# Batch 0's first MLP pass in another order, with three squares on GpSimd ahead of its loads

## The chip, the cores and the metric

The kernel runs on one core of a Trainium2 chip. The metric is the device time of one execution in microseconds (us); smaller is better. The engines are TensorE (PE in the profile; PEld is its weight load), VectorE (DVE), ScalarE (ACT), GpSimd (POOL) and SyncE (SP). Each works through its own instructions in the order in which they were recorded, and waits for the others through semaphores.

## The reference

A chunked attention (4 batches, 8 heads, 768 rows of 64) feeds an MLP with a snake activation on all 3072 tokens of width 512; the inner width is 2048.

```python
for c in range(nc):                       # 24 chunks of 32 queries, context 16 left, 8 right, 8 memory rows
    scores = scale * np.matmul(q_c, k_full.transpose(0, 1, 3, 2))
    ...
    out[:, :, c_start:c_end] = np.matmul(a, v_full)
...
h = x @ w_in
s = np.sin(alpha * h)
g = h + s * s / (alpha + 1e-09)
return (g @ w_out).astype(np.float32)
```

## The kernel before

The work runs in five stages. Stage -1 makes the attention of batch 0. Stage i (0 to 3) computes the MLP of batch i and, beside it, the attention of batch i+1. Nothing is scheduled at run time: the order is written out by hand in `WORDS`, one string of short words for each stage, and each word records its instructions at the end of the queues of the engines it uses. This case is about `WORDS[1]`, that is stage 0, up to the first scores of batch 1.

The MLP of a batch has two passes. The first pass makes 16 tiles of `gT`, each 128 of the 2048 inner columns for 768 tokens. For tile a the words are:

- `b a` and `h a`: the tile's eight matmuls (line 471, 128x384, in two halves of four) into a pair of PSUM banks; `h` then issues the sine on ScalarE (line 486, into a buffer `u`).
- `q aV`, `q aA`, `q aP`: the square of the sine on VectorE (line 494), ScalarE (line 491) or GpSimd (line 494), into a buffer `s2`.
- `g a`: the finish on VectorE (line 498), which writes the tile of `gT` and gives the two banks back.

The second pass is a series of matmuls of `gT` with `w_out_sb` (line 509, 128x512). Word `f n` takes the next n of them from a feed; they are used as fillers of PE. `o8` puts them in the feed in groups of eight: the first 16 are tiles 0 to 7 for token block 0 and then for block 1, so the third needs rows of `w_out` that belong to tile 2 and the fifth those of tile 4. While not all 16 tiles are finished, the feed gives 16 at the most.

Batch 1's attention needs q and k with the head dimension on the partitions. `l hp` and `k hp` turn one head pair on PE (line 322, 12 transposes of 128 columns) into one bank, and `L hp`, `K hp` copy it out on the engine that the last letter names (lines 342 and 333). `s61` is the first pair of score matmuls (line 428), `v0` the first value matmuls (line 457).

The loads of this stage are issued by GpSimd: `I7g` (w_in, line 250), `Uxy` (tiles x to y-1 of `w_out`, line 256; digits above 9 are letters, so `Ube` is tiles 11 to 13), `dq108` and `dk108` (q and k of batch 1, line 192), and `V158`, `V125`, `V102` (v of batch 1, lines 209 and 216). GpSimd runs its squares and issues its loads from the same queue. The loads share eight semaphores (lanes DMASW0 to DMASW7) in turn, so an issue waits until the load eight places before it has landed.

Of the kernel before, what the change touches and what calls it, by code (L numbers as in the profile page):

```python
# [26 lines left out]
    ),  # L27
    (
# [5 lines left out]
    ),  # L34
    (
# [887 lines left out]
```

## Time and profile before

| | us |
|---|---|
| median of 3 runs | 212.74 (212.47 to 213.02) |
| the profiled execution | 213.16 |
| its span, first to last instruction | 211.0 |
| PE busy in the span | 204.2 |
| ACT, DVE and POOL busy | 142.5, 139.8 and 101.4 |

The profile is of one execution, and its span leaves out 2.16 us of start and end (213.16 less 211.0). The profiled execution is 0.42 us above the median, about the spread of the runs. The granted TensorE clock was 1.000 over the span. A matmul's end is modelled, so PE counts as busy while matmuls follow each other; how closely they follow is read from the starts.

### The profile page before, as it was taken

To read this page: it belongs to the slowest core of one execution; us is meant where nothing else is said; L and a number is where in the kernel's file an instruction comes from. 1 tells how busy PE (TensorE), PEld (TensorE's weight loads), DVE (VectorE), ACT (ScalarE), POOL (GpSimd) and SP (SyncE) were. 2 spreads that over 40 slices of the span, in tenths; PEclk is the share of its full clock that TensorE was granted. 3 is DMA by queue.
4 is the path that set the end of the run, shared out by engine and by line. 5 is a ranking of instruction groups with operands and counts; after the bars stand their busy time and mean duration, and the time that the engine had idled before them with its cause. 6 is when DMAs were issued, how large, how long until landed. Compare 5 with 4: busy or idle time off the path is not lost.

```text
span 211.0 us, 4425 instructions
## 1 busy us (share of the span) xinstructions
PE 204.2 (97%) x1695; PEld 114.1 (54%) x1695; DVE 139.8 (66%) x212; ACT 142.5 (68%) x228; POOL 101.4 (48%) x144
## 2 busy tenths in 40 slices
PE   7988999999999999999999999999999999999994
PEld 2566565655455565554456555554555565554443
DVE  7688698997363669958685569887347289964011
ACT  4597798959837579969817398968765198991110
POOL 8999609497695496029991058960000023300000
PEclk9999999999999999999999999999999999999999
DMA  6999999999999699999996359999235400000312
GB/s 208 309 150 159 205 207 204 205 163 173 180 142 147 139 150 148 143 146 139 160 176 118 76 149 147 166 145 56 99 93 121 137 3 0 2 0 3 149 50 99
DMA packets 96452, 27.79 MB, mean 132 GB/s; under 512 B 84896, under 2 KB 92976, under 8 KB 96432
## 3 DMA queue, kind: packets, MB, share of 16 engines
q0 software_dynamic: 69824, 13.65, 87.2%
q1 hardware_dynamic: 25520, 12.30, 27.2%
q10 hardware_dynamic: 1088, 1.57, 2.2%
q8 instruction: 13, 0.21, 0.5%
q14 instruction: 7, 0.06, 0.1%
HBM read 29.66 MB, written 6.29 MB: 170 GB/s over the span
## 4 chain that ended last, share of the span: by engine, by line
PE 77%; DVE 9%; ACT 6%; issue 4%; DMA 2%; POOL 1%; SPq 0%; DVEq 0%; ACTq 0%
PE ps L509 40%; PE ps L471 28%; DVE gT L498 4%; PE ps L457 3%; DVE s L494 3%; PE ps L428 2%; DMA kq_f<-in_k_dram 2%; ACT u L486 2%; PE ps L409 1%; ACT qT L342 1%; PE ps L322 1%; DVE x_blk L397 1%; POOL s L494 1%; ACT s L491 1%; ACT pt L375 1%
## 5 line engine op out<-in xcount | busy, mean ns | idle before, releaser
L509 PE MATMUL ps<-w_out_sb,gT 128*128 128x512 bf16 (+2 forms) x400 | 89.1, 371 | 0.0
L471 PE MATMUL ps<-xT,w_in_sb 128*128 128x384 bf16 x512 | 86.4, 326 | 0.5 <-DVE gT L498 0.2
L498 DVE SCALAR_TENSOR_TENSOR gT<-s,inv_alpha,ps 128x768 bf16<-128x768 f32 x64 | 63.1, 1012 | 11.6 <-POOL s L494 5.3
L471 PEld LDWEIGHTS <-w_in_sb 128*128 128x128 bf16 x512 | 49.6, 98 | 35.4 <-issue 2.6
L486 ACT ACTIVATE u<-ps,alpha_sb 128x768 f32<-128x768 f32 x64 | 56.6, 895 | 17.1 <-PE ps L471 16.7
L509 PEld LDWEIGHTS <-gT 128*128 128x128 bf16 x400 | 36.6, 98 | 37.8 <-DVE gT L498 0.2
L494 POOL TENSOR_TENSOR s<-u 128x768 f32<-128x768 f32 x11 | 17.8, 1620 | 69.7 <-ACT u L486 57.6
L442 ACT ACTIVATE pt<-ps,biasm 128x256 bf16<-128x256 f32 x72 | 27.2, 489 | 10.5 <-PE ps L428 10.5
L516 DVE COPY o_sb<-ps 128x512 f32<-128x512 f32 (+1 forms) x15 | 10.1, 678 | 28.4 <-PE ps L509 26.5
L494 DVE TENSOR_TENSOR s<-u 128x768 f32<-128x768 f32 x24 | 22.9, 953 | 7.6 <-ACT u L486 7.6
L491 ACT ACTIVATE s<-u 128x768 f32<-128x768 f32 x29 | 24.2, 841 | 0.5
L397 DVE TENSOR_TENSOR x_blk<-ps,rinv 96x512 bf16<-96x512 f32 x32 | 22.0, 687 | 1.2 <-DVE rinv L396 0.2
L516 ACT COPY o_sb<-ps 128x512 f32<-128x512 f32 (+1 forms) x10 | 5.6, 562 | 22.3 <-PE ps L509 22.3
L396 DVE RECIPROCAL rinv<-ps 96x8 f32<-96x8 f32 x32 | 6.4, 199 | 13.4 <-PE ps L457 12.5
L209 POOL DMA_DIRECT2D vw<-in_v_dram x13 | 11.8, 911 | 5.3 <-PE ps L409 5.3
L275 POOL DMA_DIRECT2D kst<-in_k_dram x16 | 12.2, 762 | 1.5 <-DMA vw<-in_v_dram 1.1
L216 POOL DMA_DIRECT2D vw<-in_v_dram x13 | 12.4, 955 | 0.0
L269 POOL DMA_DIRECT2D kst<-in_k_dram x16 | 11.1, 691 | 2.0 <-DMA vw<-in_v_dram 1.1
L412 ACT COPY xT<-ps 128x384 bf16<-128x384 bf16 x11 | 5.4, 496 | 8.8 <-PE ps L409 8.7
L282 POOL DMA_DIRECT2D q_bf<-in_q_dram x12 | 10.7, 904 | 0.0
L457 PEld LDWEIGHTS <-pt 128*128 128x128 bf16 x192 | 8.2, 97 | 4.2 <-ACT pt L442 0.3
L765 ACT ACT_TABLE_LOAD x6 | 7.7, 1283 | 3.0 <-issue 2.9
(84 smaller groups left out, 139.1 us busy)
## 6 DMA issues: line engine op xcount, KB each, us to landing
out_dram<-o_sb SPq DMA_DIRECT2D x23, 256.0 KB, 2.3
q_bf<-in_q_dram POOLq DMA_DIRECT2D x12, 128.0 KB, 5.4
w_in_sb<-in_moe_w_in_dram POOLq DMA_DIRECT2D x1, 1152.0 KB, 11.2
vw<-in_v_dram POOLq DMA_DIRECT2D x8, 112.0 KB, 6.2
vw<-in_v_dram POOLq DMA_DIRECT2D x7, 128.0 KB, 6.1
kst<-in_k_dram POOLq DMA_DIRECT2D x14, 64.0 KB, 4.3
kst<-in_k_dram POOLq DMA_DIRECT2D x14, 56.0 KB, 4.6
kq_f<-in_q_dram ACTq DMA_DIRECT2D x2, 384.0 KB, 4.6
```

Of the source, the lines that this page charges most:

```text
L216: nc.gpsimd.dma_start(vw[72:128, c0:hi, 0:D], win(vflat, base + QW * c0 + 48, hi - c0, 56))
L275: nc.gpsimd.dma_start(kst[72:72 + n, j, :].rearrange("p (h d) -> p h d", d=D), k[b, :, QW * j + 48:QW * j + 48 + n, :].rearrange("h p d -> ...
L397: nc.vector.tensor_tensor(out=x_blk[:].rearrange("p g e d -> p e g d"), in0=otv[0:QW, :, :, 0:D], in1=rinv[:].unsqueeze(3).to_broadcast([Q ...
L442: nc.scalar.activation(pt[:, 0:H * QW].rearrange("p (g e c) -> p g e c", g=2, e=4)[:, :, :, 32 * m:32 * m + 32], sc[:, :, 0:4 * QW].rearra ...
L457: nc.tensor.matmul(otv[:, e, hp, :], pt[:, QW * i:QW * i + P], vws[b % 2][:, 2 * hp + e, j, 0:D + 1],)
L471: nc.tensor.matmul(t["hT"][:, hf, 0:HALF], w_in_sb[:, kt, P * t["ft"]:P * t["ft"] + P], t["xT"][:, kt, HALF * hf:HALF * hf + HALF], start= ...
L486: nc.scalar.activation(t["u"][:], t["hT"][:, :, 0:HALF], ACTF.Sin, scale=alpha_sb[:, ft:ft + 1])
L491: nc.scalar.activation(s2[:], u[:], ACTF.Square)
L494: e.tensor_tensor(out=s2[:], in0=u[:], in1=u[:], op=ALU.mult)
L498: nc.vector.scalar_tensor_tensor(out=gT[:, ft, :].rearrange("p (e c) -> p e c", e=2), in0=t["s2"][:], scalar=inv_alpha[:, ft:ft + 1], in1= ...
L509: nc.tensor.matmul(o[:, c0:c1], gT[:, ft, P * s:P * s + P], w_out_sb[:, ft, c0:c1], start=(ft == 0), stop=(ft == FT - 1),)
L516: copier(state["engines"][state["o"] % len(state["engines"])])(o_sb[:, c0:c1], o[:, c0:c1])
```

## The change

Only the first five lines of `WORDS[1]` change; the rest of the stage and all other stages keep their words. Two lines of the diff show the kind:

```diff
-        'o8 b0 h0 I7g q0V U69 U12 b1 h1 dq108 q1A b2 h2 b3 g0 h3 b4 g1 dk108 q2V g2 q3A b5 h5 h4 b6 h6 Ufg g3 '
+        'b0 h0 b3 o8 h3 I7g q3A q0V b1 h1 g0 U69 g3 q1V b2 h2 q2A b4 U12 h4 q4A dq108 b5 dk108 g1 h5 Ufg g2 g4 U01 U56 '
...
```

The tiles come in the order 0 3 1 2 4 5 6 10 7 9 13 8 11 12 15 14 (before: 0 1 2 3 5 4 6 7 10 9 8 11 13 15 12 14). GpSimd squares tiles 6, 7 and 13 (before: 4, 7 and 13). VectorE squares 4 tiles instead of 6 and ScalarE 9 instead of 7. ScalarE still makes 5 of the copies after turns, and VectorE 3. SP's queue is the same, the loads are issued in the same order, and from `f16` before the first scores on PE has the same order as before.

On GpSimd the change stands between the loads of `w_out` and v. The names are: line 256 loads of `w_out` (the fourth row below, of 2x512, is `U24`, and the later one of 512 is `U45`), lines 209 and 216 v (`V158`), line 494 a square; in brackets the semaphores it waits for. Before:

```order
L256 DMA w_out_sb<-in_moe_w_out_dram 128x512 [waits DMASW7_49]
L494 TENSOR_TENSOR s_602<-u 128x768 [waits DVE_49,Activation_49,Pool_49]
L256 DMA w_out_sb<-in_moe_w_out_dram 128x2x512 [waits DMASW0_49]
L494 TENSOR_TENSOR s_630<-u 128x768 [waits DMAHW4_49,Activation_49]
L256 DMA w_out_sb<-in_moe_w_out_dram 128x512 [waits DMASW1_49]
L209 DMA vw_89<-in_v_dram 64x24x64 [waits DMASW2_49]
L216 DMA vw_89<-in_v_dram 56x24x64 [waits DMASW3_49]
L494 TENSOR_TENSOR s_701<-u 128x768 [waits Activation_49]
L256 DMA w_out_sb<-in_moe_w_out_dram 128x3x512 [waits DMASW4_49]
```

And the same stretch of GpSimd's queue after the change:

```order
L256 DMA w_out_sb<-in_moe_w_out_dram 128x512 [waits DMASW7_49]
L494 TENSOR_TENSOR s_619<-u 128x768 [waits DMAHW2_49,Activation_49,Pool_49]
L494 TENSOR_TENSOR s_644<-u 128x768 [waits DVE_49,Activation_49]
L256 DMA w_out_sb<-in_moe_w_out_dram 128x2x512 [waits DMASW0_49]
L494 TENSOR_TENSOR s_671<-u 128x768 [waits Activation_49]
L256 DMA w_out_sb<-in_moe_w_out_dram 128x512 [waits DMASW1_49]
L209 DMA vw_89<-in_v_dram 64x24x64 [waits DMASW2_49]
L216 DMA vw_89<-in_v_dram 56x24x64 [waits DMASW3_49]
L256 DMA w_out_sb<-in_moe_w_out_dram 128x3x512 [waits DMASW4_49]
```

`U24` now stands behind the squares of tiles 6 and 7, and `U45` and `V158` behind that of tile 13, which stood behind them.

On PE the 8 turns (96 transposes) and the 16 fillers ahead of the first scores are dealt out differently. Before: 48 transposes after the 13th tile, 7 fillers 20 matmuls of tiles later, 48 transposes, 9 fillers. After: 24 transposes after the 12th tile, 24 after the 14th, then 5 fillers, 12, 12 and 24 transposes among the last two tiles, and 11 fillers. The five fillers of the change on PE, with the transposes of k ahead of them and those of q behind:

```order
L322 MATMUL ps<-ident,k_bf 64x128
L509 LDWEIGHTS gT [waits DMASW6_49]
L509 MATMUL ps<-w_out_sb,gT 128x512 [waits DVE_49]
L509 LDWEIGHTS gT
L509 MATMUL ps<-w_out_sb,gT 128x512 [waits DMASW2_49]
L509 LDWEIGHTS gT
L509 MATMUL ps<-w_out_sb,gT 128x512 [waits DMASW0_49]
L509 LDWEIGHTS gT
L509 MATMUL ps<-w_out_sb,gT 128x512
L509 LDWEIGHTS gT
L509 MATMUL ps<-w_out_sb,gT 128x512 [waits DMASW1_49]
L322 LDWEIGHTS q_bf
```

In before the same five rows, with the same waits, stand behind tile matmuls:

```order
L471 MATMUL ps<-xT,w_in_sb 128x384
L509 LDWEIGHTS gT [waits DMASW6_49]
L509 MATMUL ps<-w_out_sb,gT 128x512 [waits DVE_49]
L509 LDWEIGHTS gT
L509 MATMUL ps<-w_out_sb,gT 128x512 [waits DMASW2_49]
L509 LDWEIGHTS gT
L509 MATMUL ps<-w_out_sb,gT 128x512 [waits DMASW0_49]
L509 LDWEIGHTS gT
L509 MATMUL ps<-w_out_sb,gT 128x512
L509 LDWEIGHTS gT
L509 MATMUL ps<-w_out_sb,gT 128x512 [waits DMASW1_49]
```

What moved is their place: 124 matmuls of tiles stand ahead of the first filler before, 112 after the change, with 48 transposes ahead in both. The lane DMASW0 is that of `U24` and DMASW1 that of `U45`.

8 rows, old and new, of the table WORDS are left out of this document.

## The prediction

> **What bounds the kernel now.** I read the busy times of two stretches first, to see which engine never rests and whether a delay before the first scores of batch 1 can be made up later; then PE's timeline in the pass that changes; then GpSimd's timeline and the landing of its loads.
>
> ```profile
> 23.29:50.99 27.70, 27.53 (x241) 16.39 (x239) 24.31 (x29) 23.97 (x30) 16.99 (x20) 1.00 1.40 195
> 51.00:205.00 154.00, 153.69 (x1165) 83.30 (x1165) 96.45 (x134) 102.37 (x175) 62.16 (x72) 1.00 1.09 111
> ```
>
> Behind the stretch stands its length, then the busy time of PE (with the number of its instructions), PEld, DVE, ACT and POOL. PE is the one that never rests. From 51 to 205 us PE idles 0.31 us of 154, so what PE loses before 51 us has next to nothing to hide in: I carry it to the end in full. (Since a matmul's end is modelled, short waits are covered by its tail; but those for finishes depend on PE's own tiles and move along with them.) The stretch that changes is 23.29 to 50.99, from the tiles' matmuls to the first score matmul, 27.70 us.
>
> ```profile
> 23.29 16.91 PE L471 MATMUL ps<-xT,w_in_sb 128*128 128x384 bf16 x101
> 40.12 1.30 PE L322 MATMUL ps<-ident,q_bf 128*64 128x128 bf16 x36
> 41.23 0.53 PE L322 MATMUL ps<-ident,k_bf 128*64 128x128 bf16 x12
> 41.87 3.46 PE L471 MATMUL ps<-xT,w_in_sb 128*128 128x384 bf16 x20
> 45.17 1.67 PE L509 MATMUL ps<-w_out_sb,gT 128*128 128x512 bf16 x7
> 46.68 0.81 PE L471 MATMUL ps<-xT,w_in_sb 128*128 128x384 bf16 x4
> 47.42 0.86 PE L322 MATMUL ps<-ident,k_bf 128*64 128x128 bf16 x24
> 48.12 0.50 PE L322 MATMUL ps<-ident,q_bf 128*64 128x128 bf16 x12
> 48.45 0.50 PE L322 MATMUL ps<-ident,k_bf 128*64 128x128 bf16 x12
> 48.89 2.17 PE L509 MATMUL ps<-w_out_sb,gT 128*128 128x512 bf16 x9
> 50.99 0.51 PE L428 MATMUL ps<-qT,kT 64*128 64x96 bf16 x16
> ```
>
> Paces, from start to start. A tile matmul: the undisturbed run below of 58 lasts 9.59 us, of which 0.33 is the tail of the last, so 9.26/57 = 0.1625 us. A filler: 7 in 1.67 with a tail of 0.38, 0.215 us. A transpose: 24 in 0.86 with a tail of 0.22, 0.028 us.
>
> ```profile
> 23.78 9.59 PE L471 MATMUL ps<-xT,w_in_sb 128*128 128x384 bf16 x58
> ...
> 39.71 0.49 PE L471 MATMUL ps<-xT,w_in_sb 128*128 128x384 bf16 x2
> ```
>
> Changing the kind of matmul costs too: the two of the second row start at 39.71 and 39.87, the next could start at 40.03, and the transposes start at 40.12 (above): 0.09 us.
>
> The 27.70 us are then 125 tile matmuls x 0.1625 = 20.31, 96 transposes x 0.028 = 2.69, 16 fillers x 0.215 = 3.44: 26.44 us of bare work. The other 1.26 us are 7 changes of kind (0.63) and 0.63 us of waits. Of these the run of 101 holds 0.33 (16.91 less the tail is 16.58, against 100 x 0.1625 = 16.25), where a tile waits for two banks from a finish; most of the rest lies at 41.87, where a tile waits for a bank of q turns to be copied out (12 transposes from 41.23 and a change end at 41.66). So the order has at the most 0.63 us of waiting to give, 0.3% of the time.
>
> **The loads that the fillers need.**
>
> ```profile
> 21.26 0.90 POOL L192 DMA_DIRECT2D q_bf<-in_q_dram  x1
> 22.14 0.90 POOL L192 DMA_DIRECT2D k_bf<-in_k_dram  x1
> ...
> 24.77 1.06 POOL L256 DMA_DIRECT2D w_out_sb<-in_moe_w_out_dram x2 [1.18 <-DMA w_in_sb<-in_moe_w_in_dram]
> 31.98 1.59 POOL L494 TENSOR_TENSOR s<-u 128x768 f32<-128x768 f32 x1 [6.14 <-ACT u L486]
> 33.53 0.77 POOL L256 DMA_DIRECT2D w_out_sb<-in_moe_w_out_dram x1
> 34.39 1.46 POOL L494 TENSOR_TENSOR s<-u 128x768 f32<-128x768 f32 x1
> 35.81 0.59 POOL L256 DMA_DIRECT2D w_out_sb<-in_moe_w_out_dram x1
> 36.40 0.99 POOL L209 DMA_DIRECT2D vw<-in_v_dram x1
> 41.22 1.82 POOL L494 TENSOR_TENSOR s<-u 128x768 f32<-128x768 f32 x1 [2.83 <-ACT u L486]
> 42.99 2.12 POOL L256 DMA_DIRECT2D w_out_sb<-in_moe_w_out_dram x3
> ```
>
> These are q and k of batch 1, U01 and U56 (24.77, two issues in 1.06 us, the second at 25.3), U24 (33.53), U45 (35.81), V158 (36.40) and Ube with two more (42.99), with the three squares between. Their landings, by DMA issues of short windows in the order of issue (q, k, U01 and U56, U24, U45, V158's first, Ube; the last number is us from issue to landing, of a row with x2 the median):
>
> ```profile
> q_bf<-in_q_dram POOLq DMA_DIRECT2D x1, 768.0 KB, 15.5
> k_bf<-in_k_dram POOLq DMA_DIRECT2D x1, 768.0 KB, 18.5
> w_out_sb<-in_moe_w_out_dram POOLq DMA_DIRECT2D x2, 128.0 KB, 17.2
> w_out_sb<-in_moe_w_out_dram POOLq DMA_DIRECT2D x1, 256.0 KB, 10.9
> w_out_sb<-in_moe_w_out_dram POOLq DMA_DIRECT2D x1, 128.0 KB, 9.4
> vw<-in_v_dram POOLq DMA_DIRECT2D x1, 192.0 KB, 10.4
> w_out_sb<-in_moe_w_out_dram POOLq DMA_DIRECT2D x1, 384.0 KB, 5.6
> ```
>
> So U56 lands at about 25.3 + 17.2 = 42.5, U24 at 33.53 + 10.9 = 44.4, U45 at 35.81 + 9.4 = 45.2, V158 from 36.40 + 10.4 = 46.8. They land in the order of issue whatever the issue time: the queue is backed up by 9 to 17 us. In before the fillers start at 45.17, after U24, and the fifth needs U45 at 45.17 + 4 x 0.215 = 46.03: no wait. That is where the new order differs.
>
> **The change part by part.**
>
> *PE's order.* Up to the five fillers stand 109 tile matmuls from 23.29 on (112 less three made earlier), 48 transposes and 4 changes of kind: 23.29 + 17.71 + 1.34 + 0.36 = 42.70. I keep the 0.33 us of waits for finishes (ends: none, and 0.63): three squares stay on GpSimd, and of the others two move from VectorE to ScalarE, which are both busy for some 24 of the 27.70 us (first row), so neither chain gets clearly shorter. The fillers come up at 43.03, 2.1 us sooner than in before. The wait at 41.87 goes: the 24 turns are now followed by 16 tile matmuls, 2.6 us for two copies on two engines. All in all the stretch has the same 26.44 us of bare work, 11 changes of kind instead of 7 (0.99) and 0.33 of waits: 27.76 us, 0.06 above before, without any wait for a load.
>
> *The loads.* The third filler (rows of U24) is due at 43.03 + 0.43 = 43.46. U24's issue moves behind two squares: the second follows the ninth sine, which ends at 35.8 in before, so the issue comes at about 37.2 instead of 33.5; that is still 5 us before U56 lands, so it keeps its place in the queue. U45 moves behind the square of tile 13, now the eleventh sine (38.5 in before), so to about 38.7 + 1.6 = 40.3.
>
> ```profile
> 34.93 0.89 ACT L486 ACTIVATE u<-ps,alpha_sb 128x768 f32<-128x768 f32 x1
> 36.61 1.93 ACT L486 ACTIVATE u<-ps,alpha_sb 128x768 f32<-128x768 f32 x2
> ```
>
> When do they land? Soonest: right behind U56 at the rate at which k follows q (22.14 + 18.5 = 40.6 after 21.26 + 15.5 = 36.8: 768 KB in 3.9 us), so U24 at 42.5 + 1.3 = 43.8 and U45 at 44.5; waits of 0.34 and 0.27, 0.6 us. Latest: U24 as before, and U45 by the shortest way of a w_out load in these rows, 5.6 us from issue, at 45.9 to 46.0: waits of 0.94 and 1.1 to 1.2, 2.1 us. With both landing as before: 0.94 for U24, then the fifth filler, due at 44.4 + 0.43 = 44.83, waits 0.37 to 45.2: 1.3 us.
>
> ```profile
> 40.00:42.00 2.00, 1.88 (x51) 1.64 (x50) 1.90 (x3) 1.97 (x4) 0.78 (x1) 1.00 1.23 202
> 44.00:46.00 2.00, 2.00 (x13) 1.08 (x11) 1.90 (x4) 1.63 (x3) 2.00 (x3) 1.00 2.34 141
> ```
>
> Between them the last column, GB/s, falls from 202 to 141 while V158's small pieces run beside U24 and U45. V158 is now issued about 4.5 us later, which can only help those two; I take 44.3 and 45.0, nearest to their own rows: waits of 0.84 and 0.27, 1.1 us.
>
> *What I cost at nothing.* q is needed after 93 tile matmuls, at about 38.7, and lands at 36.8; k is needed 12 transposes ahead of the fillers, at 42.7, and lands at 40.6: 2 us of cover each (k had 0.6 before, at 41.23). U56, Ube and what follows keep their place in the queue, with Ube issued at about 43 as before. V158 lands up to 4.6 us later, at 51.4, and the first value matmuls come at 58.43. The last three copies of k are all on ScalarE now (0.8 us each, 2.3 in all) beside 11 fillers (2.4 us); then the exponentials may start some 0.4 us later behind the first scores than now, and the next scores, 16 fillers on (55.00), have 0.86 us of cover behind exponentials that end at 51.84 + 2.30 = 54.14.
>
> ```profile
> 55.00 0.68 PE L428 MATMUL ps<-qT,kT 64*128 64x96 bf16 x24
> ...
> 58.43 0.41 PE L457 MATMUL ps<-vw,pt 128*128 128x65 bf16 x8
> ```
>
> ```profile
> 49.01 1.51 ACT L333 COPY kT<-ps 128x768 bf16<-128x768 bf16 x2
> ...
> 51.84 2.30 ACT L442 ACTIVATE pt<-ps,biasm 128x256 bf16<-128x256 f32 x6
> ```
>
> *The sum.* +0.06 for the order and +1.1 for the loads, about +1.2 us of 213.16; against the median of 212.74 (0.2% below the profiled execution) that is 213.9.
>
> **A rule of the skill against the rows.** The rows above give 9.4 to 10.9 us from issue to landing for 128 and 256 KB. The Trainium skill, "DMA: Bandwidth & Descriptors", section "Anatomy of one DMA — SWDGE (gpsimd) path", puts a load from GpSimd at about 2.0 us plus its bytes at 436 KB per us. By that rule U24 would be there 2.6 us after 37.2 and U45 2.3 us after 40.3, both before PE asks, and the sum would be +0.06. The trace does not agree while the queue is full; the second rival is this case, by rows.
>
> **The rivals.**
>
> *The forecast: PE waits for U24 and U45.* For it: landings in order behind a full queue, and PE 2.1 us early. +0.7 to +1.4 us, 213.4 to 214.1.
>
> *The loads are in time.* The transfers ahead would have to drain faster, or PE come later, so that U24 lands by 43.5 and U45 by 43.9. Against it: q to U24 have the same order and the same start. Then only the order counts: +0.06, 212.8.
>
> *U45 is issued too late.* If the queue runs dry on some of its engines before 40.3 + 5.6, U45 takes its own way from the issue: 2.1 + 0.06, 214.9. Against it: U24 alone keeps the queue filled to 43.8.
>
> *Faster: turns hide in the tiles.* Transposes spread among tiles might cost nothing at a change of kind and take up the waits for finishes. Then nearly all of the 1.26 us of changes and waits go, to 0.33: -0.9 us, 211.8. It decides only if U24 lands by 43.5 too, and the change at 40.12 speaks against it.
>
> **How the numbers follow.** The forecast has 0.68, loads in time 0.17, U45 late 0.08, faster 0.07. 0.3% is 0.64 us, about what a measurement of this kernel tells from no change: slower means above 213.38. The forecast's low end lies at that bound, which gives 0.02 of it to "same": slower 0.74, same 0.19, faster 0.07. The range of 212.6 to 214.9 takes in the second case and reaches the third.
>
> **What would show it.** PE's timeline should show five L509 at about 43 us with a gap of 0.3 to 1.0 us before the third, released by a w_out load, and a smaller one before the fifth; U24 issued at about 37 and landing near 44.3; the first L428 at about 52.2 instead of 50.99; and all after it shifted by the same 1.2 us. I am wrong if the third filler starts without a gap, or if PE reaches the fillers after 44 us because the finishes have become the slower chain, or if later stages take up the delay.

## The result: slower by 0.7%, and the profile after

| | before | after |
|---|---|---|
| median of 6 runs each, us | 212.98 (212.47 to 213.31) | 214.38 (214.06 to 215.4) |
| ratio to before | 1 | 1.0072 (95%: 1.0046 to 1.0098) |
| span of the profiled execution, us | 211.0 | 213.3 |
| first score matmul minus first matmul of the run of 93 or 101, us | 27.71 | 29.13 |

The profiled execution of the changed kernel is the longest of its six (215.4 us). It reaches the pass at 24.23 us instead of 23.29 because a value matmul of stage -1 waits 1.0 us for a load of v, ahead of anything that the change touches. So stage times are compared from the start of the pass here, and a second profile of the same kernel stands below. (Lengths of the pass are taken from unrounded starts and can differ from the rows by 0.01 us.) Two of the six executions of one version below, before with U45 issued late, count as slow and are left out of its median and ratio, though their granted clock, 0.992, is that of three of the four that are kept.

The two stretches of after, as read for before (length, then busy time of PE, PEld, DVE, ACT and POOL):

```profile
24.23:53.36 29.13, 28.00 (x240) 16.10 (x240) 22.61 (x26) 25.70 (x33) 16.37 (x20) 1.00 1.35 186
53.37:205.00 151.63, 150.02 (x1137) 82.17 (x1154) 95.66 (x133) 102.25 (x174) 63.10 (x73) 1.00 1.09 110
```

The pass is 1.42 us longer, and PE idles 1.13 us of it, where before it idled 0.17. (About 0.2 of the 1.13 is a matmul without a record, see below; in the second stretch more of PE's records are missing, so its busy time says less than the starts do.) PE's timeline in the pass says where:

```profile
24.23 15.61 PE L471 MATMUL ps<-xT,w_in_sb 128*128 128x384 bf16 x93
39.77 0.86 PE L322 MATMUL ps<-ident,q_bf 128*64 128x128 bf16 x24
40.56 2.77 PE L471 MATMUL ps<-xT,w_in_sb 128*128 128x384 bf16 x16
43.27 0.53 PE L322 MATMUL ps<-ident,q_bf 128*64 128x128 bf16 x12
43.62 0.50 PE L322 MATMUL ps<-ident,k_bf 128*64 128x128 bf16 x12
44.06 0.61 PE L509 MATMUL ps<-w_out_sb,gT 128*128 128x512 bf16 x2
44.95 0.38 PE L509 MATMUL ps<-w_out_sb,gT 128*128 128x512 bf16 x1 [0.29 <-DMA w_out_sb<-in_moe_w_out_dram]
46.05 0.38 PE L509 MATMUL ps<-w_out_sb,gT 128*128 128x512 bf16 x1 [0.73 <-DMA w_out_sb<-in_moe_w_out_dram]
...
50.88 2.55 PE L509 MATMUL ps<-w_out_sb,gT 128*128 128x512 bf16 x10
53.36 0.51 PE L428 MATMUL ps<-qT,kT 64*128 64x96 bf16 x16
```

Five fillers are recorded by the kernel here and four shown: the fourth has no record. The third could have started at 44.06 + 2 x 0.2155 = 44.49 and started at 44.95; the fifth could have started at 44.95 + 0.43 = 45.38 and started at 46.05. The two waits are 0.46 and 0.67 us, 1.13 together. (The brackets give the idle time behind the modelled end, so they read less for the third, and more for the fifth, whose neighbour is missing.) GpSimd's timeline, and the landings of U24, U45 and the first of V158, by DMA issues of a short window each:

```profile
34.30 1.52 POOL L494 TENSOR_TENSOR s<-u 128x768 f32<-128x768 f32 x1 [7.54 <-issue]
36.62 1.47 POOL L494 TENSOR_TENSOR s<-u 128x768 f32<-128x768 f32 x1 [0.80 <-ACT u L486]
38.03 0.77 POOL L256 DMA_DIRECT2D w_out_sb<-in_moe_w_out_dram  x1
39.83 1.46 POOL L494 TENSOR_TENSOR s<-u 128x768 f32<-128x768 f32 x1 [1.02 <-ACT u L486]
41.24 0.59 POOL L256 DMA_DIRECT2D w_out_sb<-in_moe_w_out_dram  x1
41.83 0.98 POOL L209 DMA_DIRECT2D vw<-in_v_dram  x1
```

```profile
w_out_sb<-in_moe_w_out_dram POOLq DMA_DIRECT2D x1, 256.0 KB, 6.9
w_out_sb<-in_moe_w_out_dram POOLq DMA_DIRECT2D x1, 128.0 KB, 4.8
vw<-in_v_dram POOLq DMA_DIRECT2D x1, 192.0 KB, 5.6
```

U24 is issued at 38.03 and lands at 44.9, U45 at 41.24 and 46.0: PE's third and fifth filler start within 0.1 us of these landings. From the first scores on all is equal: the first value matmuls come 7.44 us behind them in both kernels, the next stage 21.96 and 21.97 us behind them, the one after that 46.59 and 46.58 us later, and the last another 46.18 and 46.17.

### The profile page after: what moved, and what is told of

Read it like the earlier page. It is cut to its first block, busy times and chain, and to the rows that moved or that the text cites. A ratio compares the mean times of both kernels' runs of the same rounds, so it can differ in the third digit from the quotient of the medians.

```text
span 213.3 us, 4404 instructions
## 1 busy us (share of the span) xinstructions
PE 201.6 (95%) x1674; PEld 113.2 (53%) x1695; DVE 137.5 (64%) x209; ACT 144.8 (68%) x231; POOL 102.2 (48%) x144
## 4 chain that ended last, share of the span: by engine, by line
PE 66%; POOL 11%; DMA 8%; DVE 5%; ACT 5%; issue 4%; DVEq 0%; POOLq 0%; ACTq 0%
PE ps L509 35%; PE ps L471 25%; DMA vw<-in_v_dram 8%; DVE gT L498 3%; ACT u L486 3%; PE ps L457 3%; POOL vw L209 2%; POOL vw L216 2%; PE ps L428 2%; DVE s L494 2%; ACT s L491 2%; POOL s L494 1%; POOL w_out_sb L256 1%; PE ps L409 1%; POOL kT L869 1%
## 5 line engine op out<-in xcount | busy, mean ns | idle before, releaser
L509 PE MATMUL ps<-w_out_sb,gT 128*128 128x512 bf16 (+2 forms) x381 | 86.7, 370 | 2.2 <-DMA w_out_sb<-in_moe_w_out_dram 1.0
L509 PEld LDWEIGHTS <-gT 128*128 128x128 bf16 x400 | 36.4, 98 | 38.2 <-issue 0.6
L494 POOL TENSOR_TENSOR s<-u 128x768 f32<-128x768 f32 x11 | 17.3, 1580 | 70.0 <-ACT u L486 50.4
L491 ACT ACTIVATE s<-u 128x768 f32<-128x768 f32 x32 | 26.7, 841 | 0.6
L494 DVE TENSOR_TENSOR s<-u 128x768 f32<-128x768 f32 x21 | 20.0, 953 | 7.5 <-ACT u L486 7.5
L516 ACT COPY o_sb<-ps 128x512 f32<-128x512 f32 (+1 forms) x10 | 5.6, 561 | 21.9 <-PE ps L509 21.9
L396 DVE RECIPROCAL rinv<-ps 96x8 f32<-96x8 f32 x32 | 6.4, 200 | 14.6 <-PE ps L457 12.5
L269 POOL DMA_DIRECT2D kst<-in_k_dram x16 | 11.9, 741 | 3.0 <-DMA vw<-in_v_dram 2.2
L216 POOL DMA_DIRECT2D vw<-in_v_dram x13 | 12.5, 964 | 0.0
L275 POOL DMA_DIRECT2D kst<-in_k_dram x16 | 12.3, 769 | 0.0
L457 PEld LDWEIGHTS <-pt 128*128 128x128 bf16 x192 | 8.2, 97 | 4.2 <-ACT pt L442 0.3
```

Source lines behind the costliest of these rows:

```text
L216: nc.gpsimd.dma_start(vw[72:128, c0:hi, 0:D], win(vflat, base + QW * c0 + 48, hi - c0, 56))
L457: nc.tensor.matmul(otv[:, e, hp, :], pt[:, QW * i:QW * i + P], vws[b % 2][:, 2 * hp + e, j, 0:D + 1],)
L491: nc.scalar.activation(s2[:], u[:], ACTF.Square)
L494: e.tensor_tensor(out=s2[:], in0=u[:], in1=u[:], op=ALU.mult)
L509: nc.tensor.matmul(o[:, c0:c1], gT[:, ft, P * s:P * s + P], w_out_sb[:, ft, c0:c1], start=(ft == 0), stop=(ft == FT - 1),)
L516: copier(state["engines"][state["o"] % len(state["engines"])])(o_sb[:, c0:c1], o[:, c0:c1])
```

## The experiments

In the tables "pass" is the first L428 less the start of the run of tiles, "to values" the first L457 less that L428. Ratios are to before, run on the same chip: its median was 212.98 us beside after, 212.82 to 212.85 beside the versions with several runs, and one execution of 213.28 beside the versions with one.

| | median, us (runs) | ratio (95%) | pass | to values |
|---|---|---|---|---|
| before (its profile) | 212.98 (6) | 1 | 27.71 | 7.44 |
| after | 214.38 (6) | 1.0072 (1.0046 to 1.0098) | 29.13 | 7.44 |
| after again | 214.30 (1) | | 28.96 | 7.44 |
| no early filler | 215.12 (4) | 1.0100 (1.0083 to 1.0117) | 29.71 | 7.44 |
| loads ahead of the squares | 214.05 (6) | 1.0064 (1.0049 to 1.0078) | 28.77 | 7.44 |
| loads by need | 213.07 (12) | 1.0014 (1.0000 to 1.0027) | 28.01 | 7.44 |
| two early fillers | 213.25 (11) | 1.0019 (1.0007 to 1.0031) | 28.01 | 7.44 |
| before, U45 issued late | 217.10 (4) | 1.0167 (1.0126 to 1.0207) | 27.70 | 12.22 |
| before, fillers early | 215.41 (4) | 1.0120 (1.0105 to 1.0135) | 30.44 | 7.44 |
| regrouped | 213.10 (12) | 1.0024 (1.0006 to 1.0042) | 27.55 | 7.44 |
| regrouped, 2nd and 3rd profile | 213.43, 213.49 (1 each) | | 27.56, 27.55 | 8.08, 7.99 |
| regrouped, v behind w_out | 212.64 (12) | 0.9986 (0.9975 to 0.9998) | 27.55 | 7.44 |

**After again**, the changed kernel as it is, for a second profile.

> The changed kernel once more, for a second profile. Theory: the start of the pass moves by up to 1.5 us from run to run (it lay at 22.7 to 24.2 us in seven profiles of kernels that are the same up to there), and the pass itself takes 29.1 us with two waits for loads of 1.1 us together, wherever it starts. Rival: the late start of 24.23 us in the first profile of this kernel belongs to the change, and comes again.

```profile
43.20 0.60 PE L509 MATMUL ps<-w_out_sb,gT 128*128 128x512 bf16 x2
44.02 0.59 PE L509 MATMUL ps<-w_out_sb,gT 128*128 128x512 bf16 x2 [0.22 <-DMA w_out_sb<-in_moe_w_out_dram]
45.02 0.38 PE L509 MATMUL ps<-w_out_sb,gT 128*128 128x512 bf16 x1 [0.41 <-DMA w_out_sb<-in_moe_w_out_dram]
```

The pass starts at 23.37, so the late start of the first profile was chance. The waits are 44.02 - 43.63 = 0.39 and 45.02 - 44.45 = 0.57, 0.96 us, and the pass is 0.17 shorter than in the first profile, as they are.

**No early filler**: the five fillers go to the other eleven.

```diff
-  ... g8 b12 h12 l0 k0 f5 q12A g11 ... q14V k3 f11 g14 ...
+  ... g8 b12 h12 l0 k0 q12A g11 ... q14V k3 f16 g14 ...
```

> The kernel after, with the five early fillers moved behind the last turns, to the other eleven (16 in one row). Theory (PE came to the fillers before U24 and U45 had landed; the two waits of 0.45 and 0.67 us are the loss): no filler waits for a load, the pass from the first long row of tile matmuls to the first scores takes about 28.0 us instead of 29.1, and the time is 1.1 us below the changed kernel, some 0.3 us above the kernel before. Rival 1 (the new order of squares and finishes is slower): nothing gained, 29.1 us. Rival 2 (the five groups of turns cost the loss through changes of kind): only two changes less, about 0.2 us gained.

No wait for a load is left, and yet the pass is the second longest of all. PE, and VectorE's copy that it waits for:

```profile
43.15 0.50 PE L322 MATMUL ps<-ident,k_bf 128*64 128x128 bf16 x12
45.39 0.53 PE L322 MATMUL ps<-ident,q_bf 128*64 128x128 bf16 x12 [1.74 <-DVE qT L342]
```

```profile
44.39 0.95 DVE L342 COPY qT<-ps 128x768 bf16<-128x768 bf16 x1
```

The expectation missed. The fillers, recorded between the turns, had taken a bank of PSUM of their own; without them the next turn gets the bank of the q turn ahead of it and waits until VectorE has copied that out. The fillers' place also set the order of the banks, which nothing in the edit tells. So this run does not price the load waits; the next three leave that order alone.

**Loads ahead of the squares**: U24 and U45 are issued ahead of GpSimd's square of tile 6; PE keeps its order.

```diff
-  'b6 h6 q5V q6P b10 ... b13 U24 h13 g10 q13P U45 b8 V158 ...
+  'b6 h6 q5V U24 U45 q6P b10 ... b13 h13 g10 q13P b8 V158 ...
```

> The kernel after, with U24 and U45 issued ahead of the three squares on GpSimd, so about 3 and 8 us sooner than in the changed kernel. Theory (they land in the order of a full queue, and PE is too early for that whenever they are issued): at the most the 0.45 us by which U45 landed late behind U24 comes back; U24 still lands some 1.3 to 1.8 us behind U56, the third filler still waits 0.4 us or more, time at most 0.4 us below the changed kernel. Rival (the squares ahead of the loads made them late): both waits of the fillers go, 1.1 us gained.

GpSimd issues U24 at 30.56 and U45 at 32.45, that is 7.5 and 9.4 us after the start of this pass (23.03); in after it was 13.8 and 17.0, so they are 6.3 and 7.6 us sooner. Their landings, and PE:

```profile
w_out_sb<-in_moe_w_out_dram POOLq DMA_DIRECT2D x1, 256.0 KB, 13.2
w_out_sb<-in_moe_w_out_dram POOLq DMA_DIRECT2D x1, 128.0 KB, 12.0
```

```profile
42.86 0.60 PE L509 MATMUL ps<-w_out_sb,gT 128*128 128x512 bf16 x2
43.84 0.38 PE L509 MATMUL ps<-w_out_sb,gT 128*128 128x512 bf16 x1 [0.38 <-DMA w_out_sb<-in_moe_w_out_dram]
44.49 0.38 PE L509 MATMUL ps<-w_out_sb,gT 128*128 128x512 bf16 x1 [0.28 <-DMA w_out_sb<-in_moe_w_out_dram]
```

U24 lands at 43.76, 20.73 us after the start of this pass; in after it is 44.93 - 24.23 = 20.70. An issue 6.3 us sooner brought nothing: the landing does not follow the issue, as the theory has it. U45 lands 21.42 us after the start instead of 21.81. Of the 1.13 us of waits 0.77 are left (0.55 and 0.22), and the pass is 0.36 shorter, or 0.19 against the second profile of after. That is not shown to be the price of the squares ahead of the loads. Nine of the profiles here (the two of after, and those of no early filler, loads by need, two early fillers and the four regrouped) issue a load of 128 KB at this place of the queue 17.0 us after the start, and it lands 21.3 to 22.8 us after it: the same order of queue varies by more than 0.4 us. What is left of the waits when the squares stand behind the loads, 0.77 us, belongs to the early place of the fillers.

**Loads by need**: the same number of loads at the same places in the queue, of the same sizes in the same order, but for other tiles. Tiles 0 to 6 go into the first five, tiles 7, 8 and 15 into the last two, which the early fillers don't need.

```diff
-  ... U69 ... U12 ... Ufg ... U01 U56 ... U24 ... U45 ...
+  ... U03 ... U34 ... U45 ... U56 U67 ... U79 ... Ufg ...
```

> The kernel after, with the same loads of w_out in the same places and sizes, but the tiles 0 to 4 in the first of them (where tiles 6 to 8, 1 and 15 were), so that the two loads behind the squares carry tiles 7, 8 and 15, which the early fillers do not need. PE's, VectorE's and ScalarE's queues are unchanged. Theory: no wait at the early fillers, 1.1 us gained, about 0.3 us above the kernel before. Rival (the pass is slow for its order of tiles and squares): nothing gained.

```profile
38.20 0.86 PE L322 MATMUL ps<-ident,q_bf 128*64 128x128 bf16 x24
39.00 2.77 PE L471 MATMUL ps<-xT,w_in_sb 128*128 128x384 bf16 x16
41.70 0.53 PE L322 MATMUL ps<-ident,q_bf 128*64 128x128 bf16 x12
42.06 0.50 PE L322 MATMUL ps<-ident,k_bf 128*64 128x128 bf16 x12
42.49 1.25 PE L509 MATMUL ps<-w_out_sb,gT 128*128 128x512 bf16 x4
43.68 0.53 PE L322 MATMUL ps<-ident,q_bf 128*64 128x128 bf16 x12
44.13 2.12 PE L471 MATMUL ps<-xT,w_in_sb 128*128 128x384 bf16 x12
...
50.67 0.51 PE L428 MATMUL ps<-qT,kT 64*128 64x96 bf16 x16
```

The five fillers (one without a record) take 42.49 to 43.68 with no wait, and the pass falls to 28.01: 1.12 us less than after and 0.95 less than after again, just the two waits of each (1.13 and 0.96). Everything else of after, its queues and squares too, is unchanged, so what the load waits cost is shown: about 1.0 to 1.1 us. What is left of the change, its order alone, is 28.01 - 27.71 = +0.30 us; the runs give +0.14% (0.00 to 0.27%).

**Two early fillers**: the three that need U24 or U45 go to the later group.

```diff
-  ... l0 k0 f5 q12A ... k3 f11 g14 ...
+  ... l0 k0 f2 q12A ... k3 f14 g14 ...
```

> The kernel after with only two early fillers (tiles 0 and 1, whose loads have landed) and 14 late ones, instead of 5 and 11; loads, squares and tiles as in the changed kernel, and the two still take a bank of their own ahead of the turn that waited 1.74 us in e1. Theory (loss = fillers that ask for U24 and U45 too soon): no wait for a load, first row of tile matmuls to first scores 28.1 us, time 1.1 us below the changed kernel, 0.1% to 0.2% above the kernel before. Rival (late issue of U45 and V158 costs by itself, wherever the fillers stand): 0.5 us or less gained.

```profile
42.82 0.60 PE L509 MATMUL ps<-w_out_sb,gT 128*128 128x512 bf16 x2
43.35 0.53 PE L322 MATMUL ps<-ident,q_bf 128*64 128x128 bf16 x12
```

The same 28.01 without touching a load, and no filler waits. Two ways of taking the waits off agree to 0.01 us.

**Before, U45 issued late**: before's order on PE, with U45 and V158 behind GpSimd's square of tile 13.

```diff
-  ... g6 h9 U45 b8 h8 g7 g10 q8A q9V V158 b11 h11 ... q13P k2 q11V Ube ...
+  ... g6 h9 b8 h8 g7 g10 q8A q9V b11 h11 ... q13P U45 V158 k2 q11V Ube ...
```

> The kernel before, with U45 and V158 issued behind the square of tile 13 (at about 43 us instead of 35.8), as the change orders them; PE's queue unchanged. Theory (a load keeps its place in the queue, but one issued when the queue ahead is nearly drained takes its own way, 4.8 us in the changed kernel): U45 lands at about 47.8, the fifth filler, due at 46.0, waits 1 to 1.8 us, time 0.4% to 0.8% above before. Rival (landing follows the order alone): U45 lands at 45.2, no wait, same time as before.

The expectation missed in its place. U45, issued at 42.87, is there 2.8 us later (first row), and the early fillers don't wait; but every load behind it goes out late too. GpSimd issues Ube, U9b and Uef from 45.43 on instead of 42.99, which is 2.5 us later in the pass. U9b, the second of them (at about 46.2), lands 8.8 us later, at 55.0 (second row), and there PE waits for it after the first scores (third):

```profile
w_out_sb<-in_moe_w_out_dram POOLq DMA_DIRECT2D x1, 128.0 KB, 2.8
```

```profile
w_out_sb<-in_moe_w_out_dram POOLq DMA_DIRECT2D x1, 256.0 KB, 8.8
```

```profile
55.03 4.71 PE L509 MATMUL ps<-w_out_sb,gT 128*128 128x512 bf16 x15 [3.31 <-DMA w_out_sb<-in_moe_w_out_dram]
```

The values come 4.78 us later, the largest loss of all runs, from an issue that is 2.5 us late. Not all of it is waiting. The second filler behind the scores could have started at 51.33 + 0.2155 = 51.55 and starts at 55.03: 3.48 us. The other 1.30 us are a slower PE: its 15 fillers from 55.03 need 4.64 us up to the next scores at 59.67, where before needs 3.56 for 16 (51.44 to 55.00). The granted TensorE clock, the third number from the end of a row, says why:

```profile
52.00:54.00 2.00, 0.00 (x0) 0.00 (x0) 0.00 (x0) 2.00 (x6) 0.56 (x1) 1.00 1.74 172
55.00:57.00 2.00, 1.97 (x5) 0.69 (x5) 0.00 (x0) 0.00 (x0) 1.36 (x2) 0.50 2.74 143
```

While PE rested the clock fell to half, and the first fillers ran at that. The mean clock of the executions fits: 0.992 in five of the six, which took 216.92 to 218.27 us, and 1.000 in the sixth, which took 214.80.

The row of 2.8 us comes near what the Trainium skill, "DMA: Bandwidth & Descriptors", section "Anatomy of one DMA — SWDGE (gpsimd) path", makes of 128 KB, by estimate 2.3 us; in the other runs this load took 4.4 to 12.0 us, so there the trace does not agree.

**Before, fillers early**: before's first seven fillers 12 tile matmuls sooner.

```diff
-  ... g13 K2V h15 b12 q15V h12 ... g15 f7 h14 V125 ...
+  ... g13 K2V h15 f7 b12 q15V h12 ... g15 h14 V125 ...
```

> The kernel before, with its seven early fillers 12 tile matmuls (1.95 us) sooner, behind the 14th tile instead of ahead of the last four matmuls; tiles, squares and loads as before. Theory: PE asks for U24 at about 43.7 and for U45 at 44.1 on the profile's clock of before, and waits until about 44.4 and 45.2: 0.7 us for the third filler and 0.4 for the fifth, 1.1 us slower than before (214.0). Rival (what cost time is the new order of tiles and squares, not the place of the fillers): no change, 212.9.

Slower, but not by the loads. PE, and VectorE's copy of a k turn:

```profile
44.97 1.67 PE L509 MATMUL ps<-w_out_sb,gT 128*128 128x512 bf16 x6 [1.62 <-DVE kT L333]
```

```profile
43.97 0.95 DVE L333 COPY kT<-ps 128x768 bf16<-128x768 bf16 x1
```

The first filler gets the bank of that turn and waits 1.6 us for it, so it never gets to ask for a load early. A q turn later in the pass waits another 0.8 us, until VectorE has finished a tile. This says nothing for or against the theory; it is the lesson of the first experiment again.

**Regrouped**: the kernel with loads by need, with turns and fillers in fewer groups.

```diff
-  ... l0 k0 f5 q12A g11 L0V dy l1 b15 ... b14 k1 n1 L1V h14 k2 ... k3 f11 ...
+  ... l0 k0 l1 f4 q12A g11 L0V dy b15 ... b14 h14 L1V k1 n1 k2 ... k3 f12 ...
```

> The kernel of e3 (tiles 0 to 4 of w_out loaded first) with the turns in three groups instead of five: the third q turn beside the two before it, ahead of four early fillers instead of five, and the second k turn behind the last tile's matmuls; 12 late fillers. Theory (what e3 keeps above before is changes of kind on PE, 0.09 us into a group of transposes and 0.12 out of it): two groups less save 0.4 us, the pass takes 27.6 us against 27.7 of before and 28.0 of e3, time 0.1% to 0.2% below e3, level with before or 0.1% below. Rival (e3's rest lies in its squares and finishes): no better than e3.

```profile
42.56 0.50 PE L322 MATMUL ps<-ident,q_bf 128*64 128x128 bf16 x12
43.00 1.04 PE L509 MATMUL ps<-w_out_sb,gT 128*128 128x512 bf16 x3
43.87 2.76 PE L471 MATMUL ps<-xT,w_in_sb 128*128 128x384 bf16 x16
46.56 1.20 PE L322 MATMUL ps<-ident,k_bf 128*64 128x128 bf16 x36
```

The pass is 27.55, 0.46 us below 28.01, and 0.16 below before; but the time is not better than that of the kernel with loads by need. In this profile 0.7 us go in stage 3, where PE waits for a transposed block of x:

```profile
166.47 3.74 PE L471 MATMUL ps<-xT,w_in_sb 128*128 128x384 bf16 x22 [0.56 <-DMA xT<-x_blk]
```

To see whether that is where the gain goes, the same kernel was profiled twice more:

> The kernel of e7 once more, for a second profile: its first profile gained 0.46 us on e3 in the pass and lost 0.72 us at the fifth matmul of the last batch's first tile, which waits for a transpose by DMA (0.18 us there in before, none in e3). If that wait is chance (the chain of transposes on SP's queue takes a varying time), it is another length here, and the pass again takes 27.5 to 27.6 us; if it belongs to the order of e7, it is 0.6 to 0.8 us again.

> The same kernel as e8 for a third profile: by chance the wait at the last batch's first tile is between none and 0.8 us, by order it is 0.6 to 0.8 us; the pass takes 27.5 to 27.6 us in both cases.

The wait in stage 3 was chance: it is gone in one of the two and 0.1 us in the other. Both show another one, of which this is the first's:

```profile
53.21 2.32 PE L509 MATMUL ps<-w_out_sb,gT 128*128 128x512 bf16 x10 [0.48 <-DMA w_out_sb<-in_moe_w_out_dram]
```

The values come 0.6 us later: PE now comes to the seventh filler after the first scores before tile 14's rows are there. What the pass gains turns into a wait for the loads behind v in the queue.

**Regrouped, v behind w_out**: V158 is issued behind Uef instead of ahead of Ube, and tiles 9 to 13 are loaded in the order of need (9 to 11, then 12 and 13).

```diff
-  ... q13P Ufg b8 V158 g7 ... L3A Ube U9b q8A b11 h11 Uef q11A ...
+  ... q13P Ufg b8 g7 ... L3A U9c Uce q8A b11 h11 Uef V158 q11A ...
```

> As the regrouped kernel (turns and fillers in fewer groups, loads of w_out by need), with V158 issued behind Uef instead of ahead of the loads for tiles 9 to 15, and those split 9 to 11, 12 to 13, 14 to 15 in the order of need. Theory (the loads of one queue land in the order of issue, and what the pass gains on PE is lost to the w_out loads that stand behind v): Uef, which the seventh filler after the first scores needs at 51.8 to 52.6, now has 360 KB less ahead of it and lands 1 to 2 us sooner than its 52 to 53; no wait for w_out in or after the pass, the pass at 27.55 us and the first value matmuls 7.44 us behind the first scores. V158 lands at about 53, over 4 us ahead of the first value matmuls. Time 0.1% below before to level with it: 212.5 to 212.9 beside 212.8. Rival (the w_out loads wait for their own transfer and not for what stands ahead, or GpSimd now issues v too late): the wait of 0.4 to 0.5 us stays, or a wait for v of 0.5 to 1 us comes ahead of the first value matmuls; 213.2 to 213.8.

```profile
50.81 0.51 PE L428 MATMUL ps<-qT,kT 64*128 64x96 bf16 x16
51.25 3.63 PE L509 MATMUL ps<-w_out_sb,gT 128*128 128x512 bf16 x16
54.81 0.68 PE L428 MATMUL ps<-qT,kT 64*128 64x96 bf16 x24
```

```profile
w_out_sb<-in_moe_w_out_dram POOLq DMA_DIRECT2D x1, 128.0 KB, 6.5
```

All 16 fillers follow each other, the pass keeps its 27.55 and the values come 7.44 us behind the first scores. Uef, the load that PE waited for in the second and third profile of regrouped, is issued at 42.33 and lands 6.5 us later (last row), 25.5 us after the start of the pass; there it landed 29.9 and 29.8 us after it. It is issued 2.0 us sooner and lands 4.3 sooner, so what stands ahead of it counted too. At 0.9986 (0.9975 to 0.9998) this is the one version that is below before, by 0.3 us (0.04 to 0.53), of which the profile shows 0.15; the interval just leaves out no change.

## Why the prediction was right, step by step

*PE comes to the fillers 2.1 us sooner and waits for U24 and U45 (+1.1 us)*: shown. The five L509 started 19.83 us behind the start of the pass, against 19.74 in the prediction; U24 was issued 13.80 behind it (13.9 predicted) and U45 17.01 (17.0). The waits are 1.13 and 0.96 us in the two profiles, and with the loads' contents exchanged, or with the three fillers later, they are gone and the pass is shorter by as much. That the term came out this close is in part luck: the load at U45's place landed 21.3 to 22.8 us after the start in the nine profiles that issue it 17.0 us after it, and with a fifth filler due at 19.83 + 4 x 0.2155 = 20.69 that range would make the loss 0.6 to 2.1 us.

*How the wait divides* was off: 0.84 and 0.27 were predicted, 0.46 and 0.67 came (0.39 and 0.57 in the second profile). U24 landed 0.3 us sooner than its row in before made me take (20.7 us after the start of the pass, not 21.0); U45 landed where predicted (21.8 and 21.6, against 21.7), but since the third filler came sooner the fifth had more left to wait. The sum hangs only on the later of the two landings, so it held.

*The landing is set by the queue*: shown for U24, which an issue 6.3 us sooner didn't move. For U45, 7.6 us sooner brought 0.2 to 0.4 us, less than its landing varies between profiles with the same order, so a cost of the squares ahead of it is not shown.

*+0.06 for the order* was mis-sized: it is +0.30. The prediction priced 11 changes of kind at 0.09 us against 7 in before. By the starts in the kernel with loads by need a change into transposes costs 0.10 (39.00 + 16 x 0.1625 = 41.60, they start at 41.70), one out of them 0.13 (39.00 less 38.20 + 24 x 0.028) and 0.11 (44.13 less 43.68 + 12 x 0.028). With 26.44 us of bare work and 0.33 of waits for finishes (which after has too: 15.61 less the tail is 15.28, against 92 x 0.1625 = 14.95), 28.01 leaves 1.24 us for its 11 changes, 0.113 each. In before two of the seven lie between tiles and fillers, and these cost next to nothing: 45.17 + 7 x 0.2155 = 46.68, where the next tile matmul starts. So there are 6 more changes that cost, not 4: 6 x 0.113 = 0.68. Before's waits, as the rest of its 27.71, were 0.70 with those for finishes; 0.37 of them go, and 0.68 - 0.37 is the 0.30 within rounding. The 0.113 and the 0.70 are what is left over in two passes, so this sum had to come out; the test of it is the regrouped kernel, which has four of the 11 less, 0.45 us by this, and whose pass is 0.46 shorter.

*Everything behind the first scores is carried in full*: shown in each run whose loads behind them were in time, to 0.1 us up to the last stage, but for the chance wait of one profile in stage 3. V158 was covered: its first part landed at 41.83 + 5.6 = 47.4, 13 us ahead of the values at 60.80, and well short of the 51.4 that I allowed for. So was the copying by ScalarE.

*The rivals.* "The loads are in time" did not happen, but the two kernels without the waits are what it spoke of: 28.01, and 213.07 and 213.25 us, where it said 212.8. "U45 is issued too late" did not, since U45 took 4.8 us from its issue; its lower bound of 5.6 us was still a load behind others, as the 2.8 us show. "Turns hide in the tiles" is refuted: each change to and from transposes is paid.

*The sum*: 1.13 + 0.30 = 1.43 us, beside the 1.42 of the profile and against 1.2 predicted; the medians differ by 1.40.

What stays open: why the loads behind U45, issued 2.5 us late in before with U45 late, land up to 5 us late. U9b took 8.8 us from its issue there and 6.1 in before; what held it up was not separated. And what makes the landing at one place of the queue vary by 1.5 us from profile to profile was not tested.

## What to carry to other kernels

Moving PE's filler work forward is only worth something if its operands land sooner too: add up when the work comes due and compare it with the landing of each load, in the order of the queue, since a load behind a full queue does not land sooner for being issued sooner. Look first at which data each load holds: giving the same loads the tiles that are needed first took 1.1 us away without moving anything. And where a pass is bound by PE, count how often it changes between transposes and full matmuls (0.1 us each here), and check which buffers the moved work is given, since two of the experiments waited for a bank and not for what they were to test. A long wait of PE can cost more than its length: after one of 3.5 us the clock was at half, which took another 1.3 us.

## What the hardware showed that I had not expected

- The price of a change of kind on PE depends on the pair: 0.10 us into transposes, 0.11 to 0.13 out of them, and 0.00 to 0.05 between the 128x384 and the 128x512 matmuls.
- The landing of U45 hardly knows its issue. Counted from the start of the pass it was issued at 9.4 (loads ahead of the squares), 12.5 (before), 17.0 (after) and 19.7 us (before, U45 issued late), and landed at 21.4, 21.9, 21.8 and 22.5 us: the issue moved by 10.3 us and the landing by 1.1, so the time from issue to landing was 12.0, 9.4, 4.8 and 2.8 us. Nine profiles with one issue time, 17.0, land further apart than that: 21.3 to 22.8.
- Yet an issue 2.5 us late became 4.8 us of loss on PE for the loads behind: 3.5 of waiting, and 1.3 because the granted clock fell to 0.50 during the wait and was still there at 57 us, 2 us after PE had work again. Waits of 1.7 and 1.6 us for a bank in two other versions left the clock at 1.00.
